# Program order on four engines in the output stages of a chunked-attention and gated-MLP kernel

## The chip, the core and the metric

The kernel runs on one core of a Trainium2 chip. The metric is the device time of one execution in microseconds. Three runs of the kernel before took 934.23, 934.49 and 937.45 us; the median is 934.49 us. One more execution was recorded by the hardware profiler: it took 935.86 us, of which the instructions span 934.0 us.

## What is computed

Attention inside chunks of 64 tokens, for 8 batches x 8 heads x 576 tokens with head dimension 64, then a normalised gated MLP over the 4608 tokens (512 channels, 1536 hidden).

```python
scores = scale * np.matmul(q_c, k_c.transpose(0, 1, 2, 4, 3))   # per chunk of 64
attn = exp(scores - max) / (sum + 1e-9)
x = (attn @ v_c), heads side by side                            # 4608 x 512
xn = x / sqrt(mean(x * x) + 1e-6) * rms_g
g = xn @ w_gate
out = (g * sigmoid(g) * (xn @ w_val)) @ w_out                   # float32
```

A float32 product is made of three products of rounded parts: each operand is split into a high part (a ScalarE cast) and a low part (a VectorE subtraction), and high x high, high x low and low x high are added in PSUM.

## The kernel before

**Tiles.** The tokens are nine tiles of 512. Tiles 0, 1 and 2 are done plainly: for each of 12 slices f of the hidden dimension `gated` makes ps_g and ps_v with 12 matmuls each (line 505), a SiLU `sg` (L523), a product (L527), a high part `gh` (L528) and a low part `gl` (L532), and `down` (L540) adds 12 matmuls into the four accumulators. Tiles 3 to 8 are done as three pairs of 1024 tokens, with Strassen's scheme in Winograd's form: seven half-size products P1 to P7 in place of eight, upwards (`up_pair`, L722, six slices i) and back down (`down_pair`, L911). An output stage, called the down stage here, is one call of `down_pair`: 42 steps, seven products (order P1, P5, P2, P6, P3, P7, P4) of six slices each, and each step is six 128x512 matmuls: two each with gh x high weights, gh x low weights and gl x high weights.

**The splits of a down stage.** `split_g` makes gh (L829, ScalarE) and gl (L830, VectorE) of one step's operand. They are asked for one step ahead, and both come from a pool of two buffers each, so that the parts for step n+1 can be written only when the matmuls of step n-1 are done. In P5 and P6 VectorE also updates a running difference `tt` in each step (L856, L858). When a product's last slice is done, `finish` takes it out of PSUM, on ScalarE (P1, P5, P2) or VectorE (P6, P3, P7, P4), and P2, P3, P7 and P4 also store results to DRAM on the DMA queue of SyncE (SP). For P7 GpSimd adds, too (L887).

**Side work.** While the matmuls run, the other engines prepare what comes next, spread over steps by tables of step numbers (`Steps`). Attention of the next tokens: scores, softmax, a turn of the exponentials through DRAM (`away_e` out, `eT` back), values `ps_o` (L366), a normalisation `xu` (L380 on VectorE, L430 and L388 on ScalarE, L433 on GpSimd), a turn of the result (L394) through DRAM (`away_x` out, `x` back). In tile 2: the weight sums of the output stage, `out_sides`, for six slices (a join and four sums `wo` at L578, four casts `side` at L597, four low parts at L598, four DMAs to `osd` at L601), at steps 3i+2 to 3i+4. In tile 2 and in each down stage but the last: the seven token operands `xp` of the next pair, `x_sides` (scaling at L676 on VectorE, casts at L662 on ScalarE, low parts at L663 and differences at L679 on VectorE). In tile 0 `norm_unit` scales two attention results by 1/rms: GpSimd computes the factor `ri_u` (L470), ScalarE multiplies (L472).

**Who sets the order.** A scheduler with its own cost model orders the instructions of each engine by priority; `urgent()` raises a priority. From tile 1 on TensorE (PE) alone is held in program order (`manual_schedule`). Each engine runs its own list strictly in order and waits where the list waits. SP's list holds all the DMAs: `wr` (weights upwards, three tiles ahead), `wo` (weights downwards, 1 MB each), `qt`, `kt`, `vt`, the turns and the stores.

Of the kernel before, what the change touches and what calls it, by code (L numbers as in the profile page):

```python
# [17 lines left out]
P = 128  # L18
# [25 lines left out]
PAIR_AT = 2, 12, 21, 31  # L44
CONVS = (2,), (0, 2)
# [23 lines left out]
def tile_chunk_attn_swiglu(  # L69
# [380 lines left out]
    def norm_unit(u, banks):  # L450
# [20 lines left out]
        for s in range(2):  # L471
            nc.scalar.mul(xu[:, s], xu[:, s], ri[:, s : s + 1])  # L472
# [100 lines left out]
    def out_sides(i, st):  # L573
# [14 lines left out]
        def sums():  # L588
            total(at[2, 2], at[2, 1], at[2, 2], ALU.add)
            total(at[2, 1], at[1, 1], at[2, 1], ALU.subtract)  # L590
            total(at[1, 1], at[2, 2], at[1, 1], ALU.subtract)
            total(at[1, 2], at[1, 2], at[1, 1], ALU.subtract)

        def split():
            for p, key in ((P7, (2, 1)), (P5, (2, 2)), (P6, (1, 1)), (P3, (1, 2))):
                part = tmp.tile([P, 2, OH], F32R, tag="tmp", name="side")
                nc.scalar.copy(part[:, 0], at[key])  # L597
                nc.vector.tensor_tensor(  # L598
                    part[:, 1], at[key], part[:, 0].bitcast(F32), op=ALU.subtract
                )  # L600
                nc.sync.dma_start(out_home(i, p), part.rearrange("p a c -> p (a c)").bitcast(F32))  # L601

        return [join, sums, split]
# [53 lines left out]
    def x_side(p, src):  # L657

        t = xside[p] = big([P, 2, 2, TT], F32R, "xp")
        hi, lo = (t[:, i].rearrange("p k (n c) -> p k n c", c=2 * Q) for i in range(2))  # L660
        src = src.rearrange("p n k c -> p k n c")
        nc.scalar.copy(hi, src)  # L662
        nc.vector.tensor_tensor(lo, src, hi.bitcast(F32), op=ALU.subtract)  # L663

    xside = {}

    def x_sides(x1, x2, st):
# [3 lines left out]
        sub = ALU.subtract  # L671

        def scale(x, dts):
            for dt in dts:
                col = g_col[:, dt : dt + 1]
                nc.vector.tensor_scalar(x[:, :, dt], x[:, :, dt], col, None, op0=ALU.mult)  # L676

        def less(out, one, two):
            nc.vector.tensor_tensor(out, one, two, op=sub)  # L679

        def side_t1(p):
            x_side(p, got["t1"])

        def t1_first():
# [3 lines left out]
        got = {}  # L688
        first = [
            lambda: scale(x1, (0, 1)),  # L690
            lambda: scale(x1, (2, 3)),
        ]
        return first, [
            lambda: x_side(P1, b11),
            lambda: x_side(P2, b21),
            lambda: scale(x2, (0, 1)),
            t1_first,
            lambda: side_t1(P5),
            lambda: scale(x2, (2, 3)),
            lambda: less(got["t1"], b22, got["t1"]),  # L700
            lambda: side_t1(P6),
            lambda: x_side(P3, b22),
            lambda: less(b12, b22, b12),
            lambda: x_side(P7, b12),
            lambda: less(b21, got["t1"], b21),
            lambda: x_side(P4, b21),
        ]

# [25 lines left out]
    def up_pair(i, step, wos, tt):  # L734
# [8 lines left out]
        for k, p in enumerate(ORD if i else FIRST):  # L743
# [4 lines left out]
            for m in range(2):  # L748
# [12 lines left out]
        nc.vector.tensor_tensor(t, g[:, 0, 1], g[:, 0, 0], op=ALU.subtract)  # L761
        nc.vector.tensor_tensor(g[:, 0, 1], g[:, 1, 1], g[:, 0, 1], op=ALU.subtract)
# [62 lines left out]
    def split_g(src):  # L825
        gh = gp.tile([P, TT], F32R, name="gh")
        gl = gp.tile([P, TT], F32R, name="gl")
        with urgent():
            nc.scalar.copy(gh, src)  # L829
            nc.vector.tensor_tensor(gl, src, gh.bitcast(F32), op=ALU.subtract)  # L830
        return gh, gl

# [327 lines left out]
```

## Time and profile before

| | |
|---|---|
| Median of three runs | 934.49 us |
| Profiled execution | 935.86 us |
| its span | 934.0 us |
| TensorE busy | 892.4 us (96%) |
| VectorE, ScalarE, GpSimd busy | 637.0, 470.8, 186.7 us |
| Mean granted TensorE clock | 0.993 |
| DMA | 231.85 MB, mean 248 GB/s |

The span is cut by the matmuls into tile 0 (about 37 to 157 us), tiles 1 and 2 (to about 376), and three pairs, whose down stages begin at 505.76, 694.44 and 870.72 us. An idle time in brackets stands ahead of the instruction that ended it, with what released it. Busy time of TensorE overstates it, because a matmul's record overlaps its successor's: a 128x512 matmul has a record of 0.39 us, but twelve in a row take 2.72 us.

### The profile page before, as it was taken

How to read it: one execution, taken by the hardware profiler on the slowest of the kernel's cores; microseconds unless marked ns; L12 is line 12 of the kernel's file. 1: busy time of each engine (PE TensorE's matmuls, PEld its weight loads, DVE VectorE, ACT ScalarE, POOL GpSimd, SP SyncE). 2: the span in 40 equal slices, each digit the busy share in tenths (PEclk: the TensorE clock that was granted, in tenths of full speed). 3: DMA queues.
4: the chain of work that ended last, by engine and by line, in shares of the span. 5: the costliest groups of instructions: out<-in, count | busy, mean ns of one | idle time of the engine just before them, and what ended most of it. 6: DMA issues, size and time to landing. Idle time of an engine off the chain costs nothing.

```text
span 934.0 us, 17571 instructions
## 1 busy us (share of the span) xinstructions
PE 892.4 (96%) x6828; PEld 726.1 (78%) x6828; DVE 637.0 (68%) x1065; ACT 470.8 (50%) x779; POOL 186.7 (20%) x161
## 2 busy tenths in 40 slices
PE   5699989999999989999998999999999999999997
PEld 4478868888888778888886888888877888888786
DVE  5899983654578783975775996666859954333775
ACT  4989853443456543744453654354636632322453
POOL 0100012224300000143333001443320013332201
PEclk9999999999999999999999999999999999999999
DMA  8688998778876766677796686777777675345801
GB/s 343 243 316 303 331 325 281 244 252 249 294 288 230 229 183 202 250 276 262 237 323 241 240 331 210 283 260 241 267 273 258 241 273 229 135 153 206 340 23 69
DMA packets 85795, 231.85 MB, mean 248 GB/s; under 512 B 8912, under 2 KB 45264, under 8 KB 71504
## 3 DMA queue, kind: packets, MB, share of 16 engines
q1 hardware_dynamic: 85712, 230.72, 70.3%
q8 instruction: 54, 0.88, 0.4%
q14 instruction: 29, 0.24, 0.1%
HBM read 167.25 MB, written 63.44 MB: 247 GB/s over the span
## 4 chain that ended last, share of the span: by engine, by line
PE 76%; issue 7%; ACT 6%; DVE 6%; POOL 2%; DMA 1%; SPq 0%; DVEq 0%; ACTq 0%; POOLq 0%
PE ps_c L722 11%; PE ps_a L722 11%; PE ps_b L722 10%; PE ps_g L505 7%; PE acc L540 7%; PE ps_v L505 7%; PE ps_b L911 5%; PE ps_d L722 5%; PE ps_c L911 4%; PE ps_d L911 3%; PE ps_a L911 3%; PE ps_o L366 2%; PE ps_s L244 2%; DVE gl L830 1%; ACT w L157 1%
## 5 line engine op out<-in xcount | busy, mean ns | idle before, releaser
L722 PE MATMUL ps_b<-xp,wr 128*128 128x512 f32 x432 | 106.0, 395 | 0.0
L722 PE MATMUL ps_c<-xp,wr 128*128 128x512 f32 x432 | 104.6, 391 | 0.0
L505 PE MATMUL ps_g<-xh,parts 128*128 128x512 f32 x288 | 98.1, 400 | 5.9 <-ACT sg L523 5.1
L722 PE MATMUL ps_a<-xp,wr 128*128 128x512 f32 x432 | 103.5, 390 | 0.0
L505 PE MATMUL ps_v<-xh,parts 128*128 128x512 f32 x288 | 96.0, 393 | 0.0
L722 PEld LDWEIGHTS ps_b<-xp,wr 128*128 128x128 f32 x432 | 81.7, 190 | 17.4
L722 PEld LDWEIGHTS ps_a<-xp,wr 128*128 128x128 f32 x432 | 80.9, 188 | 16.9
L722 PEld LDWEIGHTS ps_c<-xp,wr 128*128 128x128 f32 x432 | 80.6, 188 | 17.0
L540 PE MATMUL acc<-parts,gh 128*128 128x512 f32 x288 | 90.8, 396 | 0.0
L829 ACT CAST gh<-g 128x512 fp32r<-128x512 f32 x72 | 44.6, 623 | 51.8 <-DVE gl L830 21.0
L505 PEld LDWEIGHTS ps_g<-xh,parts 128*128 128x128 f32 x288 | 55.0, 191 | 19.5 <-ACT sg L523 6.4
L505 PEld LDWEIGHTS ps_v<-xh,parts 128*128 128x128 f32 x288 | 54.7, 190 | 11.5
L540 PEld LDWEIGHTS acc<-parts,gh 128*128 128x128 f32 x288 | 53.5, 189 | 11.6 <-ACT parts L182 0.2
L801 POOL TENSOR_TENSOR g<-u,u 128x512 f32<-128x512 f32 x18 | 23.2, 1289 | 185.8 <-ACT u L769 72.1
L830 DVE TENSOR_TENSOR gl<-g,gh 128x512 fp32r<-128x512 f32 x72 | 49.3, 700 | 12.2 <-ACT gh L829 11.9
L505 PE MATMUL ps_g<-xl,parts 128*128 128x512 f32 x144 | 57.0, 396 | 0.0
L540 PE MATMUL acc<-parts,gl 128*128 128x512 f32 x144 | 56.4, 392 | 0.0
L505 PE MATMUL ps_v<-xl,parts 128*128 128x512 f32 x144 | 56.4, 392 | 0.0
L791 POOL TENSOR_TENSOR p<-p,p 128x512 f32<-128x512 f32 x36 | 46.9, 1318 | 42.8 <-DVE p L790 33.5
L769 ACT ACTIVATE p<-p 128x512 f32<-128x512 f32 x36 | 22.6, 632 | 64.4 <-POOL p L791 61.2
L433 POOL TENSOR_TENSOR ri<-ss,mhalf 128x1 f32<-128x1 f32 x32 | 19.6, 623 | 173.6 <-DVE ss L431 173.5
L527 DVE TENSOR_TENSOR sg<-ps_v,sg 128x512 f32<-128x512 f32 x36 | 24.7, 686 | 42.0 <-PE ps_v L505 35.0
(141 smaller groups left out, 1794.9 us busy)
## 6 DMA issues: line engine op xcount, KB each, us to landing
wr<-wsd SPq DMA_DIRECT2D x63, 1024.0 KB, 6.8
wo<-osd SPq DMA_DIRECT2D x30, 1024.0 KB, 7.8
raw<-w_up_dram SPq DMA_DIRECT2D x12, 1024.0 KB, 9.6
vt<-v_dram SPq DMA_DIRECT2D x18, 512.0 KB, 5.2
wsd<-parts SPq DMA_DIRECT2D x18, 512.0 KB, 7.0
qt<-qT_dram SPq DMA_DIRECT2D x17, 512.0 KB, 4.9
kt<-kT_dram SPq DMA_DIRECT2D x17, 512.0 KB, 5.8
away_e<-e SPq DMA_DIRECT2D x28, 256.0 KB, 2.4
```

Source lines behind the costliest of these rows:

```text
L244: nc.tensor.matmul(st["s"][j][c * CH : (c + 1) * CH, pr], st["q"][rows, pr, tok : tok + CH], st["k"][rows, pr, tok : tok + CH], start=True ...
L433: nc.gpsimd.tensor_tensor(ri, ss, mhalf, op=ALU.pow)
L505: nc.tensor.matmul(ps, a[f][:, cols], b[dt], start=(dt == 0 and i == 0), stop=(dt == NDT - 1 and i == 2),)
L527: nc.vector.tensor_tensor(sg, pv, sg, op=ALU.mult)
L540: nc.tensor.matmul(acc[s], a[:, cols], b, start=(f == 0 and i == 0), stop=(f == NF - 1 and i == 2),)
L722: nc.tensor.matmul(ps, w[:, a, m, cols], xp[:, b, kt], start=start and kt == 0 and i == 0, stop=stop and kt == 1 and i == 2, skip_group_ch ...
L769: nc.scalar.activation(t, t if src is None else src, AF.Silu)
L791: nc.gpsimd.tensor_tensor(kp["p5"], kp["p1"], kp["p5"], op=add)
L801: nc.gpsimd.tensor_tensor(g[:, 0, 1], kp["u2"], kept[0]["u2"], op=mult)
L829: nc.scalar.copy(gh, src)
L830: nc.vector.tensor_tensor(gl, src, gh.bitcast(F32), op=ALU.subtract)
L911: nc.tensor.matmul(banks[m][name], w[:, a, m * P : (m + 1) * P], b, start=opens and i == 0 and k == 0, stop=not (opens and p != P4) and i ...
```

## The change

The output stages are written with the splits further ahead and run with four engines in program order; side work moves to other steps; two multiplications change engine. Line numbers of the changed kernel are some 8 to 60 higher.

- `down_pair` runs inside `manual_schedule` with TensorE, ScalarE, VectorE and SP in the order of the code. GpSimd is still scheduled.
- gh is asked for two steps ahead and comes from the pool `tmp` (four buffers), gl one step ahead from its two buffers. The first two gh and the first gl are made inside the last product upwards (`first_splits`). In the last slice of a product the six matmuls are sorted so that the first half of the result ends three matmuls earlier.
- The two differences that follow an upward slice (`sum_up`) are put off to the second product of the next slice, those of the last slice to down step 1.
- `x_sides` is cut finer: operands P1, P2 and P5 are made in the down stage at the steps of `X_AT`, operands P3, P6, P7 and P4 in the first steps of the next pair (`late`). Scaling by the gain moves from VectorE to ScalarE.
- `out_sides` is spread over four steps a slice; slices 0 to 3 stay in tile 2, slices 4 and 5 move to the first pair.
- In `norm_unit` GpSimd multiplies by the factor that it has computed.
- P2's result goes to a buffer of another pool (`hold`).

```diff
+X_AT = 5, 12, 13, 14, 15, 16, 25, 27, 30
+OUT_FIRST = 4
+IN_ORDER = {
+    mybir.EngineType.PE,
+    mybir.EngineType.Activation,
+    mybir.EngineType.DVE,
+    mybir.EngineType.SP,
+}
...
-            nc.scalar.mul(xu[:, s], xu[:, s], ri[:, s : s + 1])
+            nc.gpsimd.tensor_scalar(xu[:, s], xu[:, s], ri[:, s : s + 1], None, op0=ALU.mult)
...
-        return [join, sums, split]
+        return [
+            [join, sums_one],
+            [lambda: split(P7, (2, 1)), sums_two],
+            [lambda: split(P5, (2, 2)), lambda: split(P6, (1, 1))],
+            [lambda: split(P3, (1, 2))],
+        ]
...
-                nc.vector.tensor_scalar(x[:, :, dt], x[:, :, dt], col, None, op0=ALU.mult)
+                nc.scalar.mul(x[:, :, dt], x[:, :, dt], col)
...
+        late = [
+            [lambda: less(got["t1"], b22, got["t1"]), lambda: high(P3), lambda: high(P6)],
+            [lambda: low(P6), lambda: less(b12, b22, b12), lambda: low(P3), lambda: high(P7)],
+            [lambda: low(P7), lambda: less(b21, got["t1"], b21), lambda: high(P4)],
+            [lambda: low(P4)],
+        ]
...
+            if k == 6 and last is not None:
+                with urgent():
+                    last()
...
+            if k == 1 and sums:
+                sums.pop()()
...
+    def split_high(src, ready):
+        gh = tmp.tile([P, TT], F32R, tag="tmp", name="gh")
+        nc.scalar.copy(gh, src)
+        ready.append([gh])
+
+    def split_low(src, pair):
+        gl = gp.tile([P, TT], F32R, name="gl")
+        nc.vector.tensor_tensor(gl, src, pair[0].bitcast(F32), op=ALU.subtract)
+        pair.append(gl)
...
-            split_next(n + 1)
-            gh, gl = ready.pop(n)
+            next_high(n + 2)
+            next_low(n + 1)
+            gh, gl = ready[n]
...
+            todo = [(m, k) for k in range(3) for m in range(2)]
             if i == NPR - 1:
-                with urgent():
-                    finish(p, banks, kept)
+                todo.sort()
...
-            for i in range(NPR):
-                for k, f in enumerate(out_sides(i, st)):
-                    at.setdefault(3 * i + k + 2, []).append(f)
+            for i in range(OUT_FIRST):
+                for k, todo in enumerate(out_sides(i, st)):
+                    at.setdefault(4 * i + 2 + k, []).extend(todo)
...
+            early = {n: list(todo) for n, todo in enumerate(late)}
+            for n, i in enumerate(range(OUT_FIRST, NPR)):
+                for k, todo in enumerate(out_sides(i, st)):
+                    early.setdefault(6 + 5 * n + k, []).extend(todo)
...
+        ordered.__exit__(None, None, None)
+        ordered = tc.manual_schedule(engines=IN_ORDER)
+        ordered.__enter__()
+        down_pair(t, gts, wos, step, b + 1 < NB, sums, ready)
+        ordered.__exit__(None, None, None)
+        ordered = tc.manual_schedule(engines={mybir.EngineType.PE})
+        ordered.__enter__()
```

**First place: VectorE in tile 2,** around the normalisation of the second of its four attention units (`xu` is its result, `ps_o` its values, `e` its exponentials, `side` and `wo` the weight sums). Before:

```order
L328 RECIPROCAL rs<-rs 128x8
L598 TENSOR_TENSOR side<-wo,side 128x256 x4
L578 TENSOR_TENSOR wo<-parts 128x1024
L578 TENSOR_TENSOR wo<-wo 128x256 x4
L380 TENSOR_TENSOR xu<-ps_o,rs 128x16x32 x2
L431 TENSOR_SCALAR ss<-ss 128x1 x2
L394 STREAM_TRANSPOSE xu<-xu 128x1024
```

The changed kernel at the same unit:

```order
L336 RECIPROCAL rs<-rs 128x8
L607 TENSOR_TENSOR side<-wo,side 128x256
L388 TENSOR_TENSOR xu<-ps_o,rs 128x16x32 x2
L439 TENSOR_SCALAR ss<-ss 128x1 x2
L402 STREAM_TRANSPOSE xu<-xu 128x1024
L607 TENSOR_TENSOR side<-wo,side 128x256 x2
```

Three of the four low parts, the join and the four sums no longer stand ahead of the normalisation.

**Second place: VectorE where the first down stage begins.** `p` minus `ps_d` belongs to the last upward product, `tt` and `g` are the put-off differences, `xu` an attention result, `xp` token operands of the next pair. Before:

```order
L803 TENSOR_TENSOR p_5269<-p_5269,ps_d 128x512
L762 TENSOR_TENSOR g<-g 128x512
L394 STREAM_TRANSPOSE xu<-xu 128x1024
L803 TENSOR_TENSOR p_5271<-p_5271,ps_d 128x512
L830 TENSOR_TENSOR gl<-g,gh 128x512
L663 TENSOR_TENSOR xp<-x,xp 128x1024
L830 TENSOR_TENSOR gl<-g,gh 128x512 x2
```

The changed kernel at the same place:

```order
L831 TENSOR_TENSOR p_5267<-p_5267,ps_d 128x512
L402 STREAM_TRANSPOSE xu<-xu 128x1024
L831 TENSOR_TENSOR p_5269<-p_5269,ps_d 128x512
L866 TENSOR_TENSOR gl<-g,gh 128x512
L787 TENSOR_TENSOR tt<-g 128x512
L788 TENSOR_TENSOR g<-g 128x512
L866 TENSOR_TENSOR gl<-g,gh 128x512 x3
```

The low part shown singly is the stage's third: the first two (one row, `gl` x2) stand eight rows further up, among the last upward slice's work. The differences now stand behind the third, and the token operands are gone from there.

**Third place: SP and TensorE towards the end of the first down stage.** `out_dram<-u` are the stores of P3's result, `wr` the first weights of the next pair. SP before:

```order
L836 DMA wo<-osd_170 128x2048
L212 DMA qt<-qT_dram 128x1024
L714 DMA wr<-wsd_140 128x2048
L213 DMA kt<-kT_dram 128x1024
L214 DMA vt<-v_dram 128x1024
L714 DMA wr<-wsd_141 128x2048
L864 DMA out_dram<-u_5784 128x512
L864 DMA out_dram<-u_5786 128x512
L714 DMA wr<-wsd_142 128x2048
L836 DMA wo<-osd_171 128x1024
```

SP in the changed kernel:

```order
L856 DMA wo<-osd_170 128x2048
L901 DMA out_dram<-u_5783 128x512
L901 DMA out_dram<-u_5785 128x512
L733 DMA wr<-wsd_140 128x2048
L733 DMA wr<-wsd_141 128x2048
L733 DMA wr<-wsd_142 128x2048
L856 DMA wo<-osd_171 128x1024
```

The next pair's first weights now stand behind the stores of P3. TensorE in the changed kernel, at the last step of P7 (`ps_b`) and the first of P4 (`ps_d`):

```order
L950 MATMUL ps_b<-gh,wo 128x512 x2
L741 MATMUL ps_a<-xp,wr 128x512
L950 MATMUL ps_b<-gl,wo 128x512
L950 MATMUL ps_b<-gh,wo 128x512 x2
L950 MATMUL ps_b<-gl,wo 128x512
L950 MATMUL ps_d<-gh,wo 128x512 x4
```

A matmul of the next pair, which needs `wr`, now stands inside the down stage; four more stand inside P4. Before, all of them stood behind the stage's last matmul.

More of the change, by code (lines that the diff above doesn't have):

```diff
@@ L655, in big @@
         return wts.tile(shape, dtype, tag="wts", name=name)
[L657 to L663, printed above, removed]
     xside = {}
@@ L732, in hold, with up_pair @@
         return xs.tile([P, TT], F32, tag="xs", name=name)
-    def up_pair(i, step, wos, tt):
+    def up_pair(i, step, wos, tt, sums, last=None):
         g = big([P, 2, 2, TT], F32, "g")
@@ L905, in down_pair @@
                 ring_load_ahead(0)
[L906 to L907 removed]
+            next_high(n + 2)
+            next_low(n + 1)
+            gh, gl = ready[n]
             w = wos[n // PER][:, n % PER]
[L909 to L921 removed]
+            todo = [(m, k) for k in range(3) for m in range(2)]
+            if i == NPR - 1:
+                todo.sort()
+            for m, k in todo:
+                nc.tensor.matmul(
+                    banks[m][name],
+                    w[:, (0, 1, 0)[k], m * P : (m + 1) * P],
+                    (gh, gh, gl)[k],
+                    start=opens and i == 0 and k == 0,
+                    stop=not (opens and p != P4) and i == NPR - 1 and k == 2,
+                    skip_group_check=True,
+                )
+            if i == NPR - 1:
+                finish(p, banks, kept)
+            if n == 1:
+                sums.pop()()
             step()
@@ L1089, in tile_chunk_attn_swiglu @@
         t = PLAIN + 2 * b
-        at = {}
+        at = early
+        early = {}
         if b + 1 < NB:
@@ L1095, in tile_chunk_attn_swiglu, with first_splits @@
                     at.setdefault(max(PAIR_AT[n] + PAIR_STEPS[k], 0), []).append(f)
-            first, both = x_sides(x, x2, st)
-            for n, f in enumerate(first):
+            one, two, late = x_sides(x, x2, st)
+            for n, f in enumerate(one[:2]):
                 at.setdefault(PAIR_AT[1] + PAIR_STEPS[-1] + 4 + n, []).append(f)
-            for n, f in enumerate(both):
-                at.setdefault(7 * NPR + 6 + 5 * n // 2, []).append(f)
+            for n, f in zip(X_AT, one[2:] + two[:1] + two[4:] + two[1:4]):
+                at.setdefault(7 * NPR + n, []).append(f)
+            early = {n: list(todo) for n, todo in enumerate(late)}
         step = Steps(at)
-        gts, wos, tt = [], [], []
+        gts, wos, tt, sums, ready = [], [], [], [], []
+        def first_splits():
+            for g, _ in gts[:2]:
+                split_high(g[:, 0, 0], ready)
+            split_low(gts[0][0][:, 0, 0], ready[0])
         for i in range(NPR):
-            gts.append(up_pair(i, step, wos, tt))
+            last_part = first_splits if i == NPR - 1 else None
+            gts.append(up_pair(i, step, wos, tt, sums, last_part))
         loaded[0] = 0
-        down_pair(t, gts, wos, step, b + 1 < NB)
+        ordered.__exit__(None, None, None)
[5 more added lines that the diff above has]
+        ordered.__enter__()
     ordered.__exit__(None, None, None)
```

116 lines of the change are left out of this document (54 added, 62 removed).

## The prediction

> **What bounds the kernel now.** I read the busy times first, then the waits of TensorE, then the windows around each wait. The first row gives busy time, share of the span and instruction count per engine:
>
> ```profile
> PE 892.4 (96%) x6828; PEld 726.1 (78%) x6828; DVE 637.0 (68%) x1065; ACT 470.8 (50%) x779; POOL 186.7 (20%) x161
> ```
>
> TensorE is the bound in every stage: VectorE, next, has almost a third of the span free. The change takes away no matmul, so it can win only time in which TensorE idles or runs at a lower clock. The waits of TensorE behind the start (waiting engine and line, what released it, total us, times, longest):
>
> ```profile
> PE ps_a L911 <- DVE gl L830: 6.0, 7, 1.6
> ...
> PE ps_g L505 <- ACT sg L523: 5.1, 3, 3.3
> ...
> PE ps_o L366 <- issue: 2.0, 1, 2.0
> PE ps_o L366 <- DMA eT<-away_e: 1.9, 2, 1.6
> ...
> PE ps_o L366 <- DVE rs L326: 0.9, 1, 0.9
> ```
>
> That is 15.9 us in all. The change touches four of the rows; "issue", TensorE waiting for nothing that the profile shows, is not touched. The first row belongs to the down stages. To size those stages whole, these are the windows of the first two (start:end, length, busy us of TensorE, weight loads, VectorE, ScalarE, GpSimd, then the granted clock, the DMA share, GB/s), and the first and last matmuls of the third, which ends with the kernel's last matmul:
>
> ```profile
> 505.76:566.85 61.09, 58.61 (x254) 46.89 (x252) 55.52 (x76) 34.07 (x54) 6.54 (x5) 1.00 0.72 258
> 694.44:756.64 62.20, 58.95 (x253) 46.76 (x253) 55.71 (x77) 34.98 (x56) 7.45 (x5) 1.00 0.64 224
> ```
>
> ```profile
> 550.42 8.16 PE ps_b L911 x36
> ```
>
> ```profile
> 870.72 1.07 PE L911 MATMUL ps_a<-gh,wo 128*128 128x512 f32 x4
> ...
> 928.42 0.61 PE L911 MATMUL ps_d<-gl,wo 128*128 128x512 f32 x2
> ```
>
> The middle fence is a row of the chain that ended last: 36 matmuls back to back take 8.16 us, 0.2267 each. A stage's 252 would take 57.12. The excess is 61.09 - 57.12 = 3.97 and 62.20 - 57.12 = 5.08; the third stage runs from 870.72 to 928.42 + 2 x 0.2267 = 928.87, which is 58.15, an excess of 1.03. Together 10.08. More than TensorE's wait row (6.0) counts: the rest is small steps between matmuls whose operands are just late.
>
> Some idles cost a second time, through the granted clock (last but two of the columns):
>
> ```profile
> 131.50:136.50 5.00, 4.71 (x14) 3.71 (x15) 4.49 (x5) 3.11 (x5) 0.00 (x0) 0.66 1.05 321
> 331.00:334.50 3.50, 3.37 (x127) 2.94 (x127) 3.18 (x12) 1.12 (x2) 0.00 (x0) 0.52 0.62 224
> 498.40:502.00 3.60, 3.48 (x9) 2.74 (x10) 1.13 (x3) 1.45 (x4) 0.00 (x0) 0.53 0.99 419
> 698.00:704.00 6.00, 3.21 (x13) 2.01 (x12) 6.00 (x7) 2.20 (x3) 1.61 (x1) 1.00 0.72 254
> ```
>
> Behind three idles the clock fell: lost time (1 - 0.66) x 5.0 = 1.7, (1 - 0.52) x 3.5 = 1.7, (1 - 0.53) x 3.6 = 1.7 us. In the second down stage (fourth row) it did not.
>
> **A. Tile 0, the multiplications on GpSimd.** The rows around the stall, with the idle ahead of an instruction and its releaser in brackets:
>
> ```profile
> 126.55 3.94 POOL L470 TENSOR_TENSOR ri_u<-ss_u,mhalf 128x2 f32<-128x2 f32 x1 [41.45 <-DVE ss_u L468]
> 130.53 0.72 ACT L472 ACTIVATE x<-x,ri_u 128x512 f32<-128x512 f32 x1 [4.50 <-POOL ri_u L470]
> 131.16 0.58 ACT L523 ACTIVATE sg<-ps_g 128x512 f32<-128x512 f32 x1
> 131.78 0.50 PE L505 MATMUL ps_g<-xh,parts 128*128 128x512 f32 x1 [3.33 <-ACT sg L523]
> 147.18 1.03 PE L488 MATMUL ps_x<-ident,x 128*128 128x128 f32 x8
> ```
>
> ScalarE waits 4.50 us for GpSimd's factor, and the SiLU that frees ps_g stands behind that wait. Once GpSimd multiplies, ScalarE can do sg as soon as its own list allows, near the 126 us at which it went idle; TensorE asked for it at 131.78 - 3.33 = 128.45. So 3.33 and its clock loss 1.7 go: gain 5.0. The price of the two multiplications on GpSimd is in no row; the nearest are its 128x512 sums and its factor:
>
> ```profile
> L791 POOL TENSOR_TENSOR p<-p,p 128x512 f32<-128x512 f32 x36 | 46.9, 1318 | 42.8 <-DVE p L790 33.5 <-DVE ss L431 7.9 <-issue 1.5
> L433 POOL TENSOR_TENSOR ri<-ss,mhalf 128x1 f32<-128x1 f32 x32 | 19.6, 623 | 173.6 <-DVE ss L431 173.5
> ```
>
> Two cost 2 x 1.32 = 2.6 (same shape, so the one I take) to 2 x 3.94 = 7.9 us. Both end before 139, and TensorE reads x only at 147.18: covered, nothing. Without that cover the price would be the same 2.6 to 7.9.
>
> **B. Tile 2, the weight sums spread.** VectorE's list ahead of the normalisation, and TensorE's idles that follow:
>
> ```profile
> 309.00 1.94 PE L366 MATMUL ps_o<-vt,eT 64*32 64x64 f32 x126 [0.88 <-DVE rs L326]
> 310.38 1.38 DVE L598 TENSOR_TENSOR side<-wo,side 128x256 fp32r<-128x256 f32 x4
> 311.79 1.23 DVE L578 TENSOR_TENSOR wo<-parts 128x1024 f32<-128x1024 f32 x1
> 313.05 1.81 DVE L578 TENSOR_TENSOR wo<-wo 128x256 f32<-128x256 f32 x4
> 314.77 1.28 DVE L380 TENSOR_TENSOR xu<-ps_o,rs 128x512 f32<-128x512 f32 x2
> ...
> 330.70 2.42 PE L366 MATMUL ps_o<-vt,eT 64*32 64x64 f32 x126 [1.55 <-DMA eT<-away_e]
> 337.34 0.50 PE L505 MATMUL ps_g<-xh,parts 128*128 128x512 f32 x1 [0.59 <-ACT sg L523]
> ```
>
> The order now has one low part (a quarter of 1.38) where 1.38 + 1.23 + 1.81 stood: xu comes about 4 us earlier, and the turn behind it, whose eT was 1.55 late, is early by 2. The idles 0.88 + 1.55 + 0.59 = 3.0 and the clock loss of 1.7 make 4.7. I take 3.9: the wait for rs comes before the moved rows, and I keep most of it (0.8).
>
> The trace has an idle of 1.55 ahead of a clock of 0.52, and one of 2.0 (issue) ahead of 0.53. [...]
>
> Slices 4 and 5 of the sums move to the first pair: 2 x (1.23 + 1.81 + 1.38) = 8.8 us of VectorE work beside upward matmuls.
>
> **C. The down stages.** VectorE where the first one begins, and two places near its end:
>
> ```profile
> 507.50 0.69 DVE L762 TENSOR_TENSOR g<-g 128x512 f32<-128x512 f32 x1 [2.13 <-POOL g L795]
> ...
> 510.44 2.31 DVE L663 TENSOR_TENSOR xp<-x,xp 128x1024 fp32r<-128x1024 f32 x1
> 512.67 1.28 DVE L830 TENSOR_TENSOR gl<-g,gh 128x512 fp32r<-128x512 f32 x2
> ...
> 543.50 1.28 DVE L830 TENSOR_TENSOR gl<-g,gh 128x512 fp32r<-128x512 f32 x2
> ...
> 560.60 3.49 DVE L830 TENSOR_TENSOR gl<-tt,gh 128x512 fp32r<-128x512 f32 x3
> ```
>
> VectorE stands 2.13 us at a difference that waits for GpSimd, then does a transposition, and 2.31 us of token operands ahead of the low parts that TensorE wants. In the new order the first two low parts are made inside the last upward slice, the differences stand behind the third, and the operands are gone. With gh two steps ahead (2 x 1.36 us) a low part of 0.64 has room for a finish of 1.28 in front. I let 0.5 of excess stay in each stage: 10.08 - 1.5 = 8.6 gained. The last step's sorted matmuls let the first half of the last result end three matmuls (0.68) sooner; it overlaps the rest of the tail:
>
> ```profile
> 928.92 1.29 DVE L890 TENSOR_TENSOR p<-p,ps_d 128x512 f32<-128x512 f32 x2 [1.67 <-PE ps_d L911]
> 929.63 1.08 SPq L864 DMA_DIRECT2D out_dram<-p  x2
> ```
>
> VectorE's half (0.64) and its store go ahead of the second half's: 0.6.
>
> The rest I cost at 0.5 together. Eight scalings a pair move to ScalarE (8 x 0.72 = 5.8, busy 34.07 of 61.09 in the stage). Operands P3, P6, P7, P4 are made in the next pair, where the fourth product is asked for 3 x 2.72 (twelve matmuls) = 8.2 us after its start; the work ahead of it is two casts and two low parts of about 1.2 each. Without that cover each late low part costs its 1.2. Putting off `sum_up` moves two differences of 0.69 behind the next product, where VectorE has a third of its time.
>
> **D. The next pair's weights, a new wait.** SP now has the first `wr` behind the stores of P3, TensorE a matmul that reads them inside the last step of P7, and strictly behind it the rest of that step and P4. The rows: P3's last matmuls, its stores, and the landing times of `wr` from 480 to 760 us:
>
> ```profile
> 549.80 0.62 PE L911 MATMUL ps_c<-gl,wo 128*128 128x512 f32 x2
> 550.95 0.94 SPq L864 DMA_DIRECT2D out_dram<-u  x2
> ```
>
> ```profile
> DMA to landing us min/median/max: 4.8/7.0/13.8
> ```
>
> Count from the stage's start S. P3 ends at 30 x 1.36 = 40.8; the stores follow 0.7 later and take 0.94, so wr issues at S + 42.5 and lands at S + 47.3, 49.5 or 56.3. TensorE wants it in step 35 behind two matmuls: S + 35 x 1.36 + 0.45 = S + 48.05. The wait is below nothing, 1.45, or 8.2. I take 1.45 at both boundaries (median): cost 2.9. Queued behind this wait are all of P4 and the finishes of P7; no one else waits.
>
> SP holds `wo` 168 to 170 behind P2's stores, too (step 17); they are wanted from step 28, 15 us later, more than the 13.8 maximum: nothing.
>
> **Sum.** 5.0 + 3.9 + 8.6 + 0.6 - 0.5 - 2.9 = 14.7 us. The profiled execution took 935.86 and would take 921.2; the median is 1.37 lower, so 934.49 becomes **919.8**.
>
> **Rivals.**
>
> The order does not do what it says: VectorE, strict now, meets the finishes (waiting for a product's end) ahead of the low parts, and the stages keep their excess of 10.1. For it: 55.5 of 61 us of VectorE are already busy, and 543.50 follows a finish directly. Against it: the rows of the start show two causes, both moved. 8.6 back: 928.4.
>
> GpSimd holds VectorE up. Two sums of GpSimd ran beside the three low parts at 560.60:
>
> ```profile
> 559.62 3.31 POOL L887 TENSOR_TENSOR p<-p,p 128x512 f32<-128x512 f32 x2 [47.96 <-DVE p L886]
> ```
>
> Three low parts took 3.49 there, where two take 1.28. If each of the four multiplications (x4 in the kernel, two units) holds VectorE 1.32 in tile 0 with TensorE behind it, 5.3 go: 925.1. Against it: VectorE has slack in tile 0. [...]
>
> Weights late. If `wr` lands at the maximum at one boundary, the wait is 8.2 and the clock falls (1.7): 8.5 more than in my sum, 928.3. At both: 936.8. It turns into **slower** when each wait is above (4.7 + 17.6) / 2 - 1.7 = 9.45, 17.6 being the sum without D: P3's finish need only be 1.6 late, as VectorE was at 560.60 (3.49 - 3 x 0.64). Then 2 x (9.8 + 1.7) = 23.0 against 17.6: 939.9. For it: three 1 MB loads are issued at once, the stores ahead of them. Against: the median, 7.0.
>
> The issue stall goes along, its place being set by the code's layout: 2.0 + 1.7 less, 916.1.
>
> **How the numbers follow.** 0.5% (4.7 us) is about what a measurement of this kernel can tell. Forecast 0.52; excess stays 0.13; GpSimd 0.07; late weights at one boundary 0.07, at both 0.09, slower 0.06; issue stall gone 0.06. At both boundaries (936.8) is within 0.5%; the rest but one is faster: 0.85, 0.09, 0.06. My own case runs from 916 (D free: 2.9 less; rs gone: 0.8 less) to 923 (half the clock and excess terms). The range takes in the cases up to 928.4 and, below, the stall gone with D half free: 914.5 to 930.
>
> **What would show it.** Right: no idle at sg in tile 0, the clock at 1.0 behind it and at 331; stages of 57.5 to 59; waits of TensorE for `wr` near 1 to 2 us at the last step of P7. Wrong: stages above 60 (excess stays), a wait for `wr` above 5 us, VectorE's low parts above 0.8 us beside GpSimd in tile 0, or a new wait for xp early in pairs two and three.

## The result and the profile after

The changed kernel took 920.56 us (median of four runs, 918.58 to 921.51) beside 935.48 us before (the three runs above and one more): ratio 0.984, 95% interval 0.981 to 0.986. Two later series of the same kernel beside the kernel before gave 0.987 (0.985 to 0.990) and 0.983 (0.982 to 0.985). The median of all 14 executions is 921.4 us; the forecast was 919.8. Between the medians of the three series lie 14.9, 11.8 and 16.4 us; all 55 executions of the kernel before have a median of 934.35, 12.9 above 921.4. The execution of it that was traced took 935.86, so a gain read from traces can come out larger than one between medians.

TensorE's busy row and its waits in the profile after, whose execution took 918.58 us, the fastest of the 14:

```profile
PE 885.6 (97%) x6828; PEld 722.1 (79%) x6828; DVE 628.7 (69%) x1041; ACT 483.8 (53%) x801; POOL 196.6 (21%) x165
```

```profile
PE ps_o L374 <- DMA eT<-away_e: 2.2, 5, 1.2
...
PE ps_g L513 <- ACT sg L531: 1.4, 2, 1.0
...
PE ps_a L950 <- DVE gl L866: 1.3, 3, 0.5
PE ps_a L741 <- DMA wr<-wsd: 0.9, 2, 0.5
```

The wait for low parts fell from 6.0 to 1.3, that for the SiLU from 5.1 to 1.4; the wait for `wr` is new (0.9 here, 0.4 and 0.3 in the two later traces); the issue row of 2.0 us is gone from this trace. One trace is not enough here, so the parts stand below for three traces of the changed kernel (spans 916.8, 920.4 and 920.3 us). Each part is cut so that it holds the same matmuls in every column, from windows and from the starts of matmuls (tile 0 ends at 154.62 before, not near 157):

| part | before | after, three traces | mean change | forecast |
|---|---|---|---|---|
| tile 0 | 117.48 | 112.90, 113.17, 112.77 | -4.5 | -5.0 |
| tile 1 | 103.62 | 104.38, 105.27, 104.05 | +0.9 | 0 |
| tile 2 | 117.33 | 111.71, 112.19, 113.38 | -4.9 | -3.9 |
| first pair upwards | 130.19 | 127.49, 130.22, 132.33 | -0.2 | +0.5 (all small waits) |
| excess of the three down stages | 10.08 | 5.12, 4.63, 4.16 | -5.4 | -8.6 + 2.9 = -5.7 |
| second and third pair upwards, same matmuls | 239.41 | 239.97, 239.80, 239.14 | +0.2 | 0 |
| last matmul's start to the end | 5.35 | 4.30, 4.29, 4.33 | -1.0 | -0.6 |
| start to the first gated matmul | 37.14 | 37.52, 37.42, 36.73 | +0.1 | 0 |
| sum | | | -14.8 | -14.7 |

The first two down stages in the first of these traces, from the first to the last of their matmuls (252, and five of the next pair):

```profile
494.00:554.33 60.33, 59.28 (x259) 47.94 (x257) 53.94 (x72) 34.00 (x56) 6.07 (x5) 1.00 0.77 275
681.19:741.39 60.20, 59.30 (x259) 47.93 (x257) 54.00 (x72) 33.99 (x56) 6.05 (x5) 1.00 0.66 244
```

With 257 x 0.2267 = 58.26 taken off, 2.07 and 1.94 us are excess, where 3.97 and 5.08 were. What is left has two main places, the start and the step with the hoisted matmul (a matmul of the next pair that now stands inside the stage). Rows of VectorE and GpSimd, then SP, then TensorE there, in the timeline:

```profile
497.12 1.30 POOL L835 TENSOR_TENSOR g<-p,p 128x512 f32<-128x512 f32 x1 [1.26 <-ACT p L797]
497.24 1.73 DVE L788 TENSOR_TENSOR g<-g 128x512 f32<-128x512 f32 x1
498.89 1.28 DVE L866 TENSOR_TENSOR gl<-g,gh 128x512 fp32r<-128x512 f32 x2
```

```profile
535.85 1.02 SPq L901 DMA_DIRECT2D out_dram<-u  x2
536.96 1.39 SPq L733 DMA_DIRECT2D wr<-wsd  x3
```

```profile
543.55 0.50 PE L741 MATMUL ps_a<-xp,wr 128*128 128x512 f32 x1 [0.52 <-DMA wr<-wsd]
```

The put-off difference `g` takes 1.73 us where others of its shape take 0.69, and the low parts behind it are late. It begins while a sum of GpSimd runs: at the nine stage starts of the three traces a put-off difference meets this sum (L835) and takes 1.59 to 1.79 us, and in eight of them TensorE then waits 0.33 to 0.48 us for a low part. `wr` is issued at 536.96, 42.96 us behind the stage's start (42.5 was the forecast), and TensorE waits for it.

Tile 0 and the start of tile 1, ScalarE, GpSimd and TensorE:

```profile
126.42 0.58 ACT L531 ACTIVATE sg<-ps_g 128x512 f32<-128x512 f32 x1
127.04 3.96 POOL L478 TENSOR_TENSOR ri_u<-ss_u,mhalf 128x2 f32<-128x2 f32 x1 [36.35 <-DVE ss_u L476]
131.10 6.99 POOL L480 TENSOR_SCALAR x<-x,ri_u 128x512 f32<-128x512 f32 x2
...
155.62 0.60 ACT L531 ACTIVATE sg<-ps_g 128x512 f32<-128x512 f32 x1 [4.63 <-DMA out_dram<-o]
156.26 0.50 PE L513 MATMUL ps_g<-xh,parts 128*128 128x512 f32 x1 [0.47 <-ACT sg L531]
```

The SiLU no longer waits for GpSimd's factor (126.42), and the multiplications end at 138.1, well ahead of the transposes. But where tile 1 begins, the SiLU now waits for the stores of tile 0's results, which hold its buffer. The tile ends 4.5 us earlier, but the four stores, issued into a stretch where the DMA engines are fully busy (share 1.08 from 150 to 155 us), now land 4.9 to 6.5 us behind their issue, in place of 2.5 to 2.7.

In tile 2 VectorE normalises directly behind one low part, and the attention's values of the next unit still find their operand a little late:

```profile
307.30 0.37 DVE L607 TENSOR_TENSOR side<-wo,side 128x256 fp32r<-128x256 f32 x1
307.59 1.28 DVE L388 TENSOR_TENSOR xu<-ps_o,rs 128x512 f32<-128x512 f32 x2
...
324.77 0.30 PE L374 MATMUL ps_o<-vt,eT 64*32 64x64 f32 x4 [1.16 <-DMA eT<-away_e]
```

### The profile page after: what moved, and what is told of

It is laid out like the page before. It is cut to its first block, busy times and chain, and to the rows that moved or that the text cites. A ratio compares the mean times of both kernels' runs of the same rounds, so it can differ in the third digit from the quotient of the medians.

```text
span 916.8 us, 17590 instructions
## 1 busy us (share of the span) xinstructions
PE 885.6 (97%) x6828; PEld 722.1 (79%) x6828; DVE 628.7 (69%) x1041; ACT 483.8 (53%) x801; POOL 196.6 (21%) x165
## 4 chain that ended last, share of the span: by engine, by line
PE 41%; DMA 4%; DVE 3%; issue 2%; POOL 1%; SPq 1%; ACT 0%; DVEq 0%; POOLq 0%
PE ps_b L741 7%; PE ps_c L741 7%; PE ps_a L741 7%; PE ps_c L950 5%; PE ps_a L950 5%; DMA wr<-wsd 4%; PE ps_b L950 4%; PE ps_d L741 4%; PE ps_d L950 2%; DVE gl L866 1%; PE ps_o L374 1%; PE ps_s L252 0%; SPq L412 0%; DVE mx L322 0%; POOL p L819 0%
## 5 line engine op out<-in xcount | busy, mean ns | idle before, releaser
L741 PE MATMUL ps_d<-xp,wr 128*128 128x512 f32 x216 | 52.2, 390 | 0.0
```

The costliest lines, as they stand in the source:

```text
L741: nc.tensor.matmul(ps, w[:, a, m, cols], xp[:, b, kt], start=start and kt == 0 and i == 0, stop=stop and kt == 1 and i == 2, skip_group_ch ...
```

## The experiments

The runs below were taken in three series, each beside the kernel before. The unaltered changed kernel had medians of 922.18 and 919.66 in two of them, so differences from its 921.4 are good to about 2 us.

**The changed kernel again,** twice, unaltered:

> The changed kernel unaltered, for a tighter ratio and a second trace. Ratio 0.983 to 0.986. If the issue idle in front of the first down stage (2.0 us before, absent in the first trace) depends on the list of TensorE, it is absent again and the time between the first upward matmul and the first down stage is 127.5 us within 0.5; if it is chance between runs, that stage differs by up to 3.5 us.

> The changed kernel unaltered, beside the two others on one chip. 920 to 923 us; the issue idle is there again, as in the second trace of this kernel (2.6 us), with a chance of four in five by the traces so far; excess of the stages near 2, 2 and 1.3 us.

Measured: 922.18 us, ratio 0.987 (0.985 to 0.990), with the issue idle (2.60 us); and 919.66 us, ratio 0.983 (0.982 to 0.985), with it (2.42 us). The first ratio lies just above its bracket, the second time just below its own (920 to 923). The first pair's upward part took 130.22 and 132.33 us beside 127.49 in the first trace. So the absence of the idle there was chance, and none of the 2.7 us between the first two traces is a gain of the change.

**The multiplications, undone and alone.** In the changed kernel back on ScalarE; in the kernel before, moved to GpSimd (the same two lines the other way round):

```diff
-            nc.gpsimd.tensor_scalar(xu[:, s], xu[:, s], ri[:, s : s + 1], None, op0=ALU.mult)
+            nc.scalar.mul(xu[:, s], xu[:, s], ri[:, s : s + 1])
```

> The changed kernel with the two multiplications of each norm_unit back on ScalarE; nothing else moves on any engine, and ScalarE's list again has x<-x,ri_u ahead of the SiLU. Theory (ScalarE's wait for GpSimd's factor held the SiLU): the idle of about 3.3 us in tile 0 returns with a granted clock near 0.66 for 5 us behind it, tiles 0 to 2 take 329.0 + 5.0 = 334 us, and the kernel is 4.5 to 5.5 us slower than the changed kernel. Rival (GpSimd's 7 us of multiplications cost VectorE as much as they free): within 1 us of the changed kernel, and VectorE's work in tile 0 is shorter by some us.

Measured: 924.60 us, ratio 0.990 (0.987 to 0.993), 2.4 us above the unaltered kernel of its series and 3.2 above 921.4, less than the 4.5 to 5.5 expected. ScalarE and TensorE in tile 0, then the windows of tile 0 (one matmul less than in the table) and tile 1:

```profile
128.98 0.72 ACT L480 ACTIVATE x<-x,ri_u 128x512 f32<-128x512 f32 x1 [4.50 <-POOL ri_u L478]
```

```profile
130.24 0.50 PE L513 MATMUL ps_g<-xh,parts 128*128 128x512 f32 x1 [2.47 <-ACT sg L531]
```

```profile
36.50:151.20 114.70, 110.16 (x720) 89.19 (x721) 100.93 (x136) 89.68 (x166) 10.73 (x6) 1.00 0.93 324
151.20:255.04 103.84, 103.84 (x817) 85.46 (x816) 53.21 (x94) 45.29 (x75) 29.79 (x24) 1.00 0.80 257
```

The idle is back, 2.47 us this time, with no lower clock behind it. With the missing matmul tile 0 takes 114.9 us, 2.0 more than the mean of 112.9 in the changed kernel; tile 1 takes what it took before (103.62, here with one matmul more), 1.0 less than in the changed kernel. So undoing the edit costs 1.0 us in the two tiles. The rest of the difference in time lies elsewhere: the first pair took 133.7 us upwards, with an issue idle of 3.69 and 6.8 us at half clock. VectorE was busy for 100.93 us in tile 0. The changed kernel's window of tile 0:

```profile
37.52:150.42 112.90, 110.68 (x721) 89.57 (x722) 103.64 (x136) 87.57 (x163) 23.12 (x10) 1.00 0.92 322
```

VectorE's same 136 instructions take 2.7 us more. Of this 1.2 stands beside GpSimd's multiplications, three subtractions of 1.6 us in place of 1.2. Another 1.1 stands beside a sum of GpSimd (L633): a low part at 144.43 takes 1.80 us in place of 0.69. In the second trace it misses that sum, and the 136 take 102.35. TensorE does not feel the multiplications; behind the long low part it waits 0.33 us, for `xl`.

> The kernel before with only the two multiplications moved to GpSimd; TensorE, VectorE and SP run the same lists as before. Theory: 4.5 to 5.5 us faster than before (ratio 0.994 to 0.995), tile 0's 3.33 us idle gone, everything else as before: down stages of 61 and 62 us, tile 2's idles of 0.88 and 1.55, and the issue idle of 2.0 us in front of the first down stage, since TensorE's list is the same. If that idle is a matter of chance between runs and not of the list, it is gone here or smaller.

Measured: 932.38 us beside 933.98, ratio 0.998 (0.996 to 0.999): 1.6 us between the medians, 2.2 by the ratio, less than the 4.5 to 5.5 expected. The same two windows, cut as in the table:

```profile
38.00:150.12 112.12, 110.65 (x721) 89.89 (x722) 102.15 (x136) 87.28 (x163) 22.98 (x10) 1.00 0.91 322
150.12:254.65 104.53, 103.93 (x816) 85.19 (x815) 51.97 (x94) 45.27 (x75) 29.91 (x24) 1.00 0.83 266
```

Tile 0 gained 117.48 - 112.12 = 5.4 us, tile 1 lost 0.9, and the issue idle (2.3 us) was there as before. What is worth 5.4 us in this pair of traces is worth about 2 in the kernel. The wait for stores accounts for 0.9 of the difference. Another 1.7 is the stretch at half clock in the trace before: the run above had the idle without it, so not every execution loses it. The rest is within what other places of a trace vary by.

**The weight sums,** all six slices back in tile 2 at three steps a slice:

```diff
-            for i in range(OUT_FIRST):
-                for k, todo in enumerate(out_sides(i, st)):
-                    at.setdefault(4 * i + 2 + k, []).extend(todo)
+            for i in range(NPR):
+                o = out_sides(i, st)
+                o = [o[0][:1], [o[0][1], o[1][1]], [o[1][0], *o[2], *o[3]]]
+                for k, todo in enumerate(o):
+                    at.setdefault(3 * i + k + 2, []).extend(todo)
...
-            for n, i in enumerate(range(OUT_FIRST, NPR)):
-                for k, todo in enumerate(out_sides(i, st)):
-                    early.setdefault(6 + 5 * n + k, []).extend(todo)
```

> The changed kernel with the weight sums of all six slices back in tile 2 at the old three steps a slice (a join, four sums, four splits). Theory (the sums ahead of the attention's normalisation made tile 2's stall): tile 2 takes 115 to 117.5 us again (117.1 before, 111.7 to 112.0 in the changed kernel), the kernel is 3.5 to 5.5 us slower than the changed one. Rival (tile 2's gain came from the token operands moved out of it, or from chance): tile 2 stays within 1 us of 112. What the two slices cost in the first pair is read from the upward part of it: less than 1 us.

Measured: 923.41 us, ratio 0.988 (0.985 to 0.991), 2.0 us above 921.4, less than the 3.5 to 5.5 expected. VectorE, and the window of tile 2:

```profile
305.71 1.38 DVE L607 TENSOR_TENSOR side<-wo,side 128x256 fp32r<-128x256 f32 x4
...
310.10 1.28 DVE L388 TENSOR_TENSOR xu<-ps_o,rs 128x512 f32<-128x512 f32 x2
```

```profile
253.54:368.42 114.88, 112.47 (x1202) 91.57 (x1200) 81.59 (x171) 64.90 (x109) 5.71 (x8) 0.99 0.72 226
```

The four low parts, the join and the sums stand ahead of the normalisation again, and tile 2 costs 114.88 us, 2.5 more than the mean of 112.4 in the changed kernel and just below the bracket. But part of this is the clock. Tile 2 ran at half clock for one stretch here, as it did before, and so it did in the third trace of the unaltered kernel; in its other two it did not. The stretch here, and in that third trace, with the third trace's tile 2:

```profile
326.31:329.72 3.41, 3.41 (x93) 2.85 (x84) 2.82 (x9) 3.39 (x5) 0.00 (x0) 0.50 0.62 222
```

```profile
325.20:328.61 3.41, 3.41 (x52) 2.66 (x34) 2.95 (x6) 3.41 (x7) 0.00 (x0) 0.50 0.56 199
253.55:366.93 113.38, 111.81 (x1201) 91.21 (x1200) 74.10 (x154) 65.67 (x104) 4.37 (x8) 0.98 0.67 211
```

Trace against trace with such a stretch, the spread of the sums is worth 114.88 - 113.38 = 1.5 us, and 117.33 - 114.88 = 2.5 of the gain is not the sums: it is what else left tile 2 (token operands, scalings on VectorE) or chance. The first pair did not gain without slices 4 and 5: 131.9 us upwards, which is 127.8 without its issue idle (2.44) and the half clock behind it (1.7), where the changed kernel has 127.5 to 128.2.

**The down stages.** First, only TensorE in program order:

```diff
 IN_ORDER = {
     mybir.EngineType.PE,
-    mybir.EngineType.Activation,
-    mybir.EngineType.DVE,
-    mybir.EngineType.SP,
 }
```

> The changed kernel with only TensorE in program order in the down stages; VectorE, ScalarE and SP are ordered by the scheduler. The splits stay as far ahead. VectorE's list has a difference and token operands ahead of the stage's first low parts again, SP's list has wr ahead of P3's stores, TensorE's list has no matmul of the next pair inside the stage. Theory (the order of the lists makes the stalls): the first two stages take 60 to 62 us for their 252 matmuls (excess 3 to 5 each, now 2.06 and 1.94), no wait for wr inside the stage, and the kernel is 1 to 5 us slower than the changed kernel. Rival (the distance of the splits makes the gain): excess below 1.5 each, kernel 0 to 2 us faster, since the waits for wr of 0.7 and 0.6 us go.

Measured: 926.31 us, ratio 0.991 (0.988 to 0.994), 4.9 us above 921.4. The first two stages (252 matmuls, no hoisted ones):

```profile
498.87:558.52 59.65, 58.23 (x254) 46.98 (x253) 52.09 (x71) 33.80 (x55) 5.71 (x5) 1.00 0.74 265
686.73:747.57 60.84, 58.48 (x254) 46.88 (x252) 52.30 (x71) 34.82 (x57) 6.99 (x6) 1.00 0.64 229
```

Excess 2.53 and 3.72 with no wait for `wr`, where the changed kernel has 1.4 to 2.1 with one. The theory had 3 to 5, its rival below 1.5, so the first stage fits neither: without the order the stages lose 0.8 and 1.9 us more. The three stages together have 7.7 us of excess, beside 4.6 in the changed kernel and 10.1 before, and make 3 of the 4.9 us.

Second, the high parts one step ahead and no splits inside the upward part, order kept:

```diff
+        next_high(0)
+        next_low(0)
         for n, (p, i) in enumerate(order):
...
-            next_high(n + 2)
+            next_high(n + 1)
             next_low(n + 1)
...
-            last_part = first_splits if i == NPR - 1 else None
+            last_part = None
```

> The changed kernel with the high parts asked for one step ahead, not two, and none of a down stage's splits made inside the last upward product; program order kept on four engines, VectorE's list at the start of the stage the same. ScalarE's list has the finish of a product ahead of the next high part. Theory (the order at the start of the stage makes the gain, the second step of distance is cover): excess of each stage 2 to 3.5 us (now 1.6 to 2.1), the kernel 0 to 4 us slower than the changed one. Rival (the distance makes the gain): excess 4 us or more in each stage, waits of TensorE for low parts at each product's first step, 6 us or more slower.

Measured: 925.22 us, ratio 0.990 (0.987 to 0.993), 3.8 us above 921.4. The first two stages with their five hoisted matmuls, and the first matmuls of P5:

```profile
496.12:558.08 61.96, 60.40 (x259) 47.47 (x257) 53.53 (x72) 33.45 (x56) 6.02 (x5) 1.00 0.73 263
685.18:747.48 62.30, 60.36 (x259) 47.47 (x258) 53.55 (x72) 33.43 (x56) 6.03 (x5) 1.00 0.64 236
```

```profile
507.34 1.20 PE L952 MATMUL ps_c<-gh,wo 128*128 128x512 f32 x4 [0.78 <-ACT gh L861]
```

Excess 3.70 and 4.04, and 9.6 us in the three stages: nearly as much as before the change (3.97 and 5.08, 10.1 in all). The excess lies between theory and rival, the time in the theory's bracket (0 to 4 us slower). TensorE now waits for a high part, which stands behind P1's finish (1.27 us) and a cast of token operands (1.05) on ScalarE, as it must in program order. Order and distance need each other: strict lists without the second step and the early splits, which this run leaves out together, give back what they gained.

Third, the two rows that were left over, moved:

```diff
-            if more and n == len(order) - 2 * NPR:
+            if more and n == len(order) - 2 * NPR - 1:
                 ring_load_ahead(0)
...
-            if n == 1:
+            if n == 3:
                 sums.pop()()
```

> The changed kernel with two rows moved: the put-off differences at down step 3 in place of 1, so that two more low parts stand ahead of them, and the next pair's first three wr ahead of P3's stores on SP. Theory: the waits for a low part at the start of each stage (0.6, 0.6, 0.5 us) and for wr near its end (0.7, 0.6) go, excess of the stages below 1.0 each, the kernel 1.5 to 3 us faster than the changed one. Rival: the differences at step 3 stand ahead of P5's low parts and the wait only moves, or the stores of P3 now late hold a buffer; excess unchanged.

Measured: 918.36 us, ratio 0.982 (0.979 to 0.986), 3.0 us below 921.4; it varied from 914.93 to 922.82, so the times alone do not part it from the changed kernel. The stages, now with one hoisted matmul (253 x 0.2267 = 57.36):

```profile
499.02:557.34 58.32, 58.18 (x254) 47.12 (x253) 52.87 (x72) 33.91 (x55) 5.17 (x4) 1.00 0.77 280
684.76:743.38 58.62, 58.46 (x254) 47.05 (x253) 53.37 (x72) 33.89 (x56) 6.50 (x5) 1.00 0.67 251
```

Excess 0.96 and 1.26 (below 1.0 was expected), and no wait of TensorE inside the stages. That names both remaining places of the changed kernel. The third stage, in which nothing waits for `wr`, shows the start alone: its excess is 1.1 us in all three traces of the changed kernel and 0.5 here. The put-off difference no longer meets GpSimd's sum and takes 0.69 us again; more low parts stand ahead of it, too, and the run does not part the two. Of the kernels tried it has the lowest median.

**The issue idle.** The values' burst of small matmuls in the pairs cut in two halves a step apart:

```diff
-PAIR_STEPS = -4, 0, 3, 5, 8, 11, 13
+PAIR_STEPS = -4, 0, 3, 5, 8, 11, 13, 7
...
+        ] + [lambda: turned_values(u, range(4))] * (u >= 6 + 4)
```

> The changed kernel with the 128 small matmuls of an attention unit's values cut in two halves in the pairs, with twelve 128x512 matmuls between them. Theory (the idle of 2.0 to 3.7 us ahead of the first down stage, named issue, comes when a burst of some 256 short instructions ends and the next 16 KB of instructions have not been fetched; it comes in some executions and not in others): no issue idle, the first pair's upward part takes 126 to 127.8 us (130.2, 130.2, 133.7 with the idle, 127.5 without), times spread less, median 1 to 3 us below the changed kernel. Rival (the idle is a wait of the matmul behind the burst for data): it stays between 2 and 4 us behind the second half.

Measured: 931.09 us, ratio 0.997 (0.995 to 0.999), 9.7 us above 921.4, where 1 to 3 below was expected: the theory in this form is refuted. The halves began a step earlier, and their operand was late (TensorE waited 4.4 us for `eT` in all). The issue idles stayed; in the second pair one stood where none had been, inside the second half:

```profile
496.89 2.57 PE L742 MATMUL ps_b<-xp,wr 128*128 128x512 f32 x10 [1.18 <-issue]
```

```profile
686.90 0.32 PE L375 MATMUL ps_o<-vt,eT 64*32 64x64 f32 x9 [1.72 <-issue]
```

In the first pair it came two matmuls behind the burst, but with as many instructions ahead of it in TensorE's list as in the other kernels (8642 in the trace, 8641 or 8642 in the others). That suggested a place in the list, not the length of a burst. So the last unit was moved away from the place, by one step or two, in the kernel with the two moved rows:

```diff
-PAIR_AT = 2, 12, 21, 31
+PAIR_AT = 2, 12, 21, 30
```

> The kernel with the differences at down step 3 and wr ahead of P3's stores, and the last attention unit of a pair one step earlier, so that twelve 128x512 matmuls stand between the end of its burst of small matmuls and the place in TensorE's list where the issue idle stood in six traces (there the 16 KB instruction fetch began as TensorE ran out). Theory (the place is fixed in the list, and a burst in front of it leaves no time for the fetch): no issue idle, or one below 0.7 us, the first pair's upward part 126 to 128 us in place of 130 to 133.7, the kernel 2 to 3.5 us faster than without the moved unit (918.4), 4 to 6.5 us faster than the changed kernel run beside it. Rival (the idle belongs to the burst and goes with it): 2 us or more behind the burst again, time as without the moved unit.

Measured: 921.62 us, ratio 0.985 (0.983 to 0.987), 2.0 us above the unaltered changed kernel beside it, where 4 to 6.5 below was expected. The burst and what follows it in the unaltered changed kernel (second trace), in its first trace, and with the unit moved by one step:

```profile
488.59 1.48 PE L374 MATMUL ps_o<-vt,eT 64*32 64x64 f32 x128
492.68 2.58 PE L741 MATMUL ps_b<-xp,wr 128*128 128x512 f32 x10 [2.60 <-issue]
```

```profile
487.01 1.48 PE L374 MATMUL ps_o<-vt,eT 64*32 64x64 f32 x128
488.42 3.02 PE L741 MATMUL ps_b<-xp,wr 128*128 128x512 f32 x12
```

```profile
488.20 1.48 PE L374 MATMUL ps_o<-vt,eT 64*32 64x64 f32 x128
489.62 3.02 PE L741 MATMUL ps_c<-xp,wr 128*128 128x512 f32 x12
```

With the unit moved the idle behind the same burst is gone, as expected of a fixed place. But the kernel gained nothing, and the first pair took 130.8 us upwards: the unit's scores, moved too, met other such places, behind 8129 and 11201 instructions of the list (512 ahead of the old place, and 2560 behind it in the second pair). TensorE's waits there:

```profile
PE ps_s L252 <- issue: 3.5, 2, 2.1
```

> The same with the last attention unit two steps earlier; its scores now stand directly behind the values of the unit before it, a burst of 384 instructions or more. Theory: no issue idle at the old place (24 matmuls, 5.4 us, in front of it); a new one only if a fetch falls into the longer burst, then up to 2 us. Otherwise as with one step. Rival: the idle stays behind the burst, 2 us or more.

Measured: 935.56 us, ratio 1.000 (0.998 to 1.002), 15.9 us above the unaltered kernel beside it. The old place was free of the idle again, but values and scores back to back waited 6.7 us for `eT`, 3.9 us for issue, and 10.2 us ran at half clock. The expectation did not see that two units now shared the same steps.

## Why the prediction was right, and where it was not

**The size and sign held,** and mostly for the reasons given: 14.7 us forecast, 14.8 in the mean of three traces, with no part off by more than 1.0 us. That it came so close is in part luck: the loss in tile 1 and the surplus in tile 2 cancel, the terms of C and D were each off by some 2.5 us in opposite directions, and the medians of the three series give 11.8 to 16.4 us.

**A, tile 0.** The idle and its cause were right: tile 0 gained 4.5 us, and with the edit undone the idle returns. Two things were not seen. The clock loss of 1.7 was counted as part of the stall, but undoing the edit gave an idle of 2.47 us without one, and 2.0 us of the 4.5 came back. Later executions of the kernel before ran at mean clocks from 0.990 to 1.000, the traced one at 0.993; 10 of the 51 were as low. And the gain was not followed into tile 1, where the SiLU now waits for stores: 0.9 given back. The two multiplications took 6.99 us here and 5.08 in the first unit, between the bounds of 2.6 and 7.9 and well above the lower one that was taken; the cover up to the transposes hid them all the same.

**B, tile 2.** The forecast 3.9 became 4.9, but only 1.5 of it is shown to be the spread of the sums. The credit for the whole stall was too high, and what the other operands gave by leaving tile 2 had been costed at nothing. An operand 1.2 us late remains, in place of 1.55, and the clock loss of 1.7, counted as gone, came back in one of the three traces.

**C and D, the down stages.** The three stages gained 5.4 where 5.7 was the sum of both terms, but the split was different. D was forecast at 1.45 us a boundary; TensorE's wait row is 0.9 us for both in the first trace, 0.4 and 0.3 in the others, so D cost about 0.5 in place of 2.9. The weights were there when they were forecast: the matmul that needs them starts at 543.55, which is 49.55 us into the stage (49.5 was the forecast). But TensorE came to it at 542.86, 48.86 us into the stage and not 48.05, because the excess of C was already behind it. C left 0.5 us of excess a stage in the forecast and more than 1 in fact, so it gained about 6.0 us in place of 8.6: the differences behind the third low part were meant to be harmless there, but meet GpSimd's sum and cost about 0.5 at each start, as moving them shows. The two errors cancel; that the sum of C and D came out within 0.3 us is luck.

**The rest and the tail.** The side work in the pairs was costed at 0.5 us. Without the issue idle and the half clock behind it the first pair takes 126.5 us upwards before and 127.5, 127.6 and 128.2 after: 1.3 us lost, which the idle's coming and going hides in the table. The tail gave 1.0, not 0.6.

**The rivals.** That the stages keep their stalls came true only where the high parts were one step ahead. That GpSimd holds VectorE up was looked for in tile 0, where beside the multiplications it cost VectorE 1.2 us and TensorE nothing; VectorE's low parts stayed at 0.70 us there. It was true of the end in another place, the starts of the down stages, where GpSimd's sum is met by a difference that the change had moved. The weights came late, but by less than 1 us. The vanished issue idle, a rival of 0.06, was true of the first trace and false of the kernel: of the eleven traces of kernels that end the unit's burst at the old step ten have it, the first of the changed kernel alone has not. (In three of the ten VectorE's `xu` is named as the releaser; but where there was no idle, the same matmul started at 488.42, ahead of `xu` at 488.51, so it does not wait for it; and the place in the list is the same.)

**Still open:** the other part of tile 2's gain, the 1.3 us lost in the first pair, and why the instruction packet came early in that one trace (see the last section).

## What to carry to other kernels

Put the stalls of the bounding engine together from the windows of each stage, since small late operands made 4 of the 10 us here that no wait row shows, and follow each gain to the next stage: part of it can become a wait for a store. Strict order on an engine pays only with operands asked for far enough ahead to cover what stands in its list: of 10.1 us of excess the two together took away 5.4, the distance alone 2.4, the order alone 0.5. Take several traces before a single vanished wait, or a loss of clock behind it, is counted as a gain.

## What the runs showed of the hardware

**Late instruction fetches stall TensorE at fixed places of its list.** In the second trace of the changed kernel no instruction packet was moved from 484 to 490.4 us, and one from 490.4 to 492.7, in the idle behind the burst; in the first trace it was moved from 485 to 487.2, ahead of the burst, and no idle followed. Rows of the DMA queues (packets, MB, share) of the second and the first:

```profile
q8 instruction: 1, 0.02, 2.6%
```

```profile
q8 instruction: 1, 0.02, 5.5%
```

Each trace has 54 such packets (before and after 0.88 MB in all, 16 KB each) for some 13850 instructions of TensorE (matmuls, weight loads and semaphore waits), one for 256. Counted in the traces, 8641 or 8642 instructions stand ahead of the idle in all ten; six further idles of the last three experiments stand behind 8129, 11201 or 11202, and 11713 or 11714, whole multiples of 256 away within one. One of the six bears the name of an operand (`eT`) and not of issue. With packets and blocks of 256 numbered in order, TensorE entered no block earlier than 2.2 us behind the start of its packet, at any of the 689 block boundaries of the thirteen traces; at the 16 idles it was 2.2 to 2.5 us, in the first trace, without the idle, 3.3. So at these places TensorE waited for the packet, 1.2 to 3.7 us. A packet started between 4.7 us before and 8.0 us after TensorE entered the block ahead of its own. That is early enough for a block of large matmuls, which lasts 29 us (128 x 0.2267), and too late behind 128 small ones in 1.48 us. What sets the start within that range, no run shows.

**The clock halves by fixed windows.** Stretches at half clock last 3.41 us (each of three in the trace before), 6.83 (with the multiplications back on ScalarE, from 490.90) or 10.24 (with the unit moved by two steps, from 460.32). In the trace before, half clock begins at 133.14, 331.12, 498.37 and 931.86 us, which is 58, 49 and 127 times 3.41 us apart. Windows of 3.41 us around the idle of tile 0 in the kernel before, and around the issue idle of the changed kernel's second trace:

```profile
129.73:133.14 3.41, 1.35 (x6) 1.13 (x7) 1.59 (x3) 2.61 (x4) 0.77 (x1) 1.00 0.87 309
133.14:136.55 3.41, 3.41 (x10) 2.63 (x9) 3.16 (x4) 1.52 (x3) 0.00 (x0) 0.50 1.07 314
```

```profile
490.90:494.31 3.41, 1.63 (x7) 1.37 (x8) 0.48 (x1) 1.78 (x5) 0.00 (x0) 1.00 0.99 410
494.31:497.72 3.41, 3.41 (x17) 2.81 (x16) 2.05 (x5) 1.26 (x3) 2.58 (x4) 1.00 0.23 90
```

A window in which TensorE was busy for 1.35 us was followed by one at exactly half clock; one with 1.63 was not, though an idle of 2.60 us lay across its beginning. In tile 2 before, 1.67 us of busy time with small matmuls in it (327.70 to 331.12) was followed by half clock all the same, behind an idle of 1.55 us. So the busy time of the window ahead does not decide it alone. Nor does the length of the idle: those of 2.0 us (issue, before) and 2.42 (issue, the changed kernel's third trace, where the next twelve matmuls took 4.60 us in place of 2.88) cost another 1.7; those of 2.47 (tile 0, multiplications back on ScalarE) and 2.60 (issue, second trace) cost nothing more.
